# A three-stage attention, expert and feed-forward kernel: reciprocals spread in two parts, rings of their own for the sums, and a list scheduler inside the kernel that sets the order of every engine

## Chip, cores and metric

The kernel runs on one core of one Trainium2 chip. The metric is device microseconds of one execution. Five engines are spoken of: TensorE (PE, whose weight loads are shown as PEld), VectorE (DVE), ScalarE (ACT), GpSimd (POOL) and SyncE (SP), which issues all the transfers.

## What is computed

Three layers follow one another. The first is an attention in which two neighbouring query rows are averaged, the second a mixture of four attention experts of which each token takes two, the third a gated feed-forward block on the token and the token before it.

```python
def _attn_ref(q, k, v):                      # q, k, v: 4 x 8 x 1152 x 64
    q_pool = q.reshape(B, H, S // 2, 2, D).mean(axis=3)
    scores = scale * np.matmul(q_pool, k.transpose(0, 1, 3, 2))
    attn = np.exp(scores - np.max(scores, axis=-1, keepdims=True))
    attn = attn / (np.sum(attn, axis=-1, keepdims=True) + 1e-09)
    return np.matmul(attn, v)
def _moe_ref(x, w_gate, wq, wk, wv, wo):     # x: 4 x 576 x 512, four experts
    topk = np.argpartition(-(x @ w_gate), 2, axis=-1)[..., :2]
    ...
    for e in range(E):                       # causal attention of head width 64
        ye = a @ v @ wo[e]
        out += mask[..., None] * w[:, :, kk:kk + 1] * ye
def _moe2_ref(x, mu_k, mu_r, w_k, w_v, w_r): # x_prev: the token before
    xk = mu_k * x + (1.0 - mu_k) * x_prev
    xr = mu_r * x + (1.0 - mu_r) * x_prev
    k = np.maximum(xk @ w_k, 0.0)
    return 1.0 / (1.0 + np.exp(-(xr @ w_r))) * (k * k @ w_v)
```

## The kernel before

The 32 heads of the first layer (4 batches of 8) run one after another. A head has nine steps. A step multiplies one block of 128 keys with the 576 pooled queries (`s1_job`, lines 781 and 782, into a tile `st` of which PSUM holds two), ACT takes the exponential into `p` (line 787, ten buffers), and some steps later PE multiplies `p` with the values (line 815, into one of four PSUM tiles named `bank`). The sums over the keys are not taken by PE block by block: POOL and DVE add the nine `p` (line 797, tiles `sg` and `sv`), DVE joins both (line 801, `sa`), and PE sums over the partitions with a matrix of ones (line 831). The row maxima of the next head come from matmuls into `bank` (line 728) that DVE reduces (line 730). The operands of a later head are transposed, split into a high and a low part and staged in `sk` (`s1_prep`), from where DMAs copy them to their places (`KK<-sk`, `QQ<-sk`).

The normalisation of a head goes through DRAM. ACT copies the sums to a row of `U` (`finish2`, line 848), two DMAs bring them to 64 partitions (`sd`, line 854), DVE takes the reciprocals (line 858), one DMA writes them to `scr` (line 859), and one DMA reads them back, spread over 128 partitions (`R`, line 863). POOL then multiplies `U` with `R` into `XT` (line 871). When both heads of a pair are in `XT`, `s2_split` has ACT copy the high part (`XH<-XT`, line 64) and DVE subtract for the low part (`XL`, line 71). The expert layer of a batch runs between the steps of the next batch's heads: projections of the values and the gate (`stv`, line 280), of queries and keys (`stq`, line 347), four masked attentions (lines 474 to 503, with their own `normaliser`, whose `R` is read by one DMA at line 254), and the output projection (`sto`, line 555). The expert layer of the last batch stands alone behind the heads, with parts of the feed-forward block between its steps. The feed-forward weights are split into high and low parts ahead of time, in 20 chunks through one buffer `w3st` (`w3_split`: loaded at line 947, split by ACT and DVE in lines 960 to 990, stored at line 993, read back later). Twelve of them go through during the heads, eight behind them. At the end come nine groups of 256 tokens: `sth` (line 1175), `str` (line 1198), `stw` (line 1211).

Order: the work is written as a list of steps (`drive`) with tasks placed between them by a table of numbers `G`. A task is a list of small pieces spread evenly between a start and an end that are counted in steps; `later(n, f)` puts `f` n steps behind. `end1` 5, for one, is how many steps behind the sums `XT` is written. What is written so is then ordered anew on every engine by the framework's own scheduler; `behind` and `high_priority` in `s1_job` tie a few matmuls together for it. The engines run their queues in order, each instruction waiting for its semaphores. `U`, `sd`, `rd` and `R` of the heads and of the experts share rings of two buffers in the pool `sm`.

Of the kernel before, what the change touches and what calls it, by code (L numbers as in the profile page):

```python
# [25 lines left out]
G = {'LAG': 4, 'LO': 2, 'nf1': 2, 'nfx': 1, 'mxA': (0, 5), 'mxB': (-1.0, 5.5), 'mxC': (-3.5, 5.0), 'prA': (0.5, 5.0), 'prB': (-1.5, 2.0), 'mx0': (-4.2, 4.0), 'mx1': (-4.2, 4.0), 'vl': (0.0, 1.5), 'vs': (5.5, 1.0), 'pr0': (-3.0, 1.0), 'pr1': (-3.0, 1.0), 'ldA': (5.5, 5.0), 'ldB': (2.5, 2.0), 'ld': (1.5, 1.0), 'm2': (2.0, 3.0), 'nm': 2, 'nm2': 1, 'dup': 1, 'mid': 1, 'bc': 1, 'end': 9, 'end1': 5, 'mid2': 2, 'end2': 4, 'spl': 9, 'gate': 8, 'gate2': 2, 'w2': (2, 30), 'w3': (7, 14), 've': 'g', 'kh0': 's', 'kh1': 's', 'qh0': 's', 'qh1': 's', 'kq': 's', 'kl': 'v', 'rs': 'v', 'rl': 'v', 'ym': 'g', 'yo': 'v', 'LGe': 'v', 'p1': (5, 5, 5, 9), 'p2': (9, 9, 9), 'p3': (2,), 'p4': (9, 9, 9, 9), 'p5': (8, 8, 8, 8), 'p6': (9, 9, 9), 'po': (2, 4, 5, 9), 'add0': 'g', 'add1': 'g', 'xt': 'g', 'u1': 's', 'u2': 's', 'y2': 'v', 'yh': 's', 'yl': 'v', 'xo': 'v', 'v2': 's', 'xh': 's', 'xl': 'v', 'vvh': 's', 'vvl': 'g', 'klo': 'v', 'HB': 2, 'PB': 10, 'GRP': (2, 5, 8), 'GA': (1, 3, 5, 7), 'blk': 1, 'm2w': 2, 'order': 2, 'kdup': 0, 'L2': 4, 'O2': 1, 'a0': (5.0, 5.0), 'a1': (2.0, 2.5), 'a2': (0.0, 1.0), 'a3': (2.0, 2.0), 'r0': 2, 'NV': 2, 'NF': 2, 'ua': 'v', 'u0': 's', 'xt0': 'g', 'w3d': 8, 'w3q': (3, 27), 'WC': 1, 'kb': 1, 'kst': 1, 'qst': 0, 'CW': 512, 'wt': 'v', 'wl': 'v', 'wa': 'v', 'WB': 1, 'mxg': 4, 'hq': 's', 'hpos': (0, 1, 11, 20)}  # L26
NEG = -1.0e30

TINY = 1.17e-9

# [6 lines left out]
class Task:  # L37


    def __init__(self, start, end, atoms):  # L40
        self.start, self.end, self.atoms, self.done = start, end, atoms, 0

    def run(self, now):
        if now <= self.start:
            return
        if callable(self.atoms):
            self.atoms = self.atoms()
        n = len(self.atoms)
        want = n if now >= self.end else math.ceil(n * (now - self.start) / (self.end - self.start))
        while self.done < min(want, n):  # L50
            self.atoms[self.done]()
            self.done += 1
# [3 lines left out]
def tile_kernel(ctx: ExitStack, tc: tile.TileContext, q, k, v, w_gate, wq, wk, wv, wo,  # L56
                mu_k, mu_r, w_k, w_v, w_r, out):
    nc = tc.nc
# [3 lines left out]
    def copy(e, dst, src):  # L62
        if e == "s":
            nc.scalar.activation(dst, src, AF.Copy)  # L64
        elif e == "v":
            nc.vector.tensor_copy(dst, src)
        else:
            nc.gpsimd.tensor_scalar(dst, src, 1.0, 0.0, op0=ALU.mult, op1=ALU.add)

    def lo_of(e, dst, src, hi):  # L70
        eng[e].tensor_tensor(dst, src, hi.bitcast(F32), op=ALU.subtract)  # L71
# [30 lines left out]
    make_identity(nc, ident)  # L102
# [53 lines left out]
    def run_later(everything=False):  # L156
        while pending:
            x = min(pending, key=lambda x: x[0])
            if x[0] > now[0]:
                if not everything:  # L160
                    return
                now[0] = x[0]
            pending.remove(x)
            x[1]()

    lagged = []

    def drive(steps, tasks, drain=False, first=0):
# [4 lines left out]
        for i, st in enumerate(steps, first):  # L173
            now[0] += 1
            if st.qk:
                st.qk()
            if st.ew:
# [59 lines left out]
    def normaliser(U, gate, name):  # L237
# [8 lines left out]
        def mid():  # L246
# [4 lines left out]
            later(G["bc"], bcast)  # L251

        def bcast():
            nc.sync.dma_start(R, bass.AP(tensor=scr.tensor, offset=scr.offset, ap=[[0, D], [1, T]]))

# [199 lines left out]
    def s2_job(pp, b, e):  # L455
# [68 lines left out]
        def finish(j):  # L524
# [6 lines left out]
            mid, R = normaliser(U, GR[:, e], name)  # L531
# [8 lines left out]
            later(G["mid2"], mid)  # L540
            later(G["end2"], end)
# [216 lines left out]
    last_qk, owed = [None], []  # L758

    def behind(ins, prev):  # L760
        if prev is not None:
            tc.add_manual_dep(ins.ins, prev.ins.name,
                              mybir.DependencyInfo(mybir.DependencyClass.NoSync, mybir.DependencyReason.DATA),
                              reason="order")
        return ins

    def s1_job(hh):
# [5 lines left out]
        def make(si):  # L773
            items = [(0, si), (1, si)] if wide else [(x // NC, x % NC) for x in (2 * si, 2 * si + 1)]

            def qk():
                st = acc["st", si] = psA.tile([P, 2, 512], F32, tag="st", name=f"st1_{hh}_{si}")
                for n, (j, c) in enumerate(items):
# [3 lines left out]
                    last_qk[0] = nc.tensor.matmul(st[:, n, :HT], KB[i][0 : D + 1, ks], QB[i][0 : D + 1, cs],  # L782
                                                  start=False, stop=True)
# [20 lines left out]
            def values():  # L804
# [6 lines left out]
                with tc.high_priority():  # L811
                    prev = last_qk[0]
                    for x in range(si, lo, -1):
                        for j in range(2):
                            prev = behind(nc.tensor.matmul(  # L815
                                a[j * D : (j + 1) * D, :HT], V[:, x, 0:D], ps[x][:, j],
                                start=si == GRP[0] and x == si, stop=si == NC - 1 and x == lo + 1), prev)
                    if si == GRP[0]:
                        while owed:
                            owed.pop(0)(prev)  # L820
                if si == NC - 1:
                    owed.append(total)
                    U = acc["U"] = sm.tile([P, T], F32, tag="U", name=f"U1_{hh}")
                    copy("s", U[:, :HT], a[:, :HT])
                    if hh == NH - 1:
                        owed.pop(0)(last_qk[0])

            def total(prev):
                s = aux()
                for j in range(2):  # L830
                    prev = behind(nc.tensor.matmul(s[j * D : (j + 1) * D, :HT], ones, sums["all"][:, j],  # L831
                                                   start=True, stop=True), prev)
                finish2(s)
# [12 lines left out]
        def finish2(s):  # L846
            U = acc["U"]
# [9 lines left out]
            def mid():  # L857
                nc.vector.reciprocal(rd, sd)
                nc.sync.dma_start(scr.rearrange("o (p i) -> (o p) i", p=D), rd)
                later(G["bc"], bcast)  # L860
# [12 lines left out]
            later(G["mid"], mid)  # L873
            later(G["end1"], end)
# [63 lines left out]
    def w3_split(first, end, pool, bufs):  # L938
        def chunk(src, n):
# [54 lines left out]
            return [ld, sp1, sp2, sp3, sp4, sp5, sp6, sp7]  # L994
# [34 lines left out]
    for hh in range(NH):  # L1029
# [16 lines left out]
        if b and h == 1:  # L1046
            tasks.append(Task(ex_[hh][2] + G["gate"] - 2, ex_[hh][2] + G["gate"] - 1, s2_gate(c)))
        if b and h in (2, 4, 5, 6):
            tasks.append(Task(at_[hh][0] + G["m2"][0], max(at_[hh][0] + G["m2"][0] + G["m2w"], ex_[hh][0] - G["m2"][1]), s2_max(c, max(h - 3, 0))))
# [17 lines left out]
    for hh in range(NH):  # L1067
        z = "0" if hh < H else "1"
        if hh + 1 < NH:
# [4 lines left out]
            tasks.append(Task(at(hh, mx[0]), e, s1_max(hh + 1)))  # L1074
            a = LAG + G["vl"][0]
            tasks.append(Task(at(hh, a), at(hh, a + G["vl"][1]), lambda hh=hh: s1_vload(hh + 1)))
        if hh + 2 < NH:
            pr = G["pr" + z] if hh > 1 else G["prB"] if hh else G["prA"]
            tasks.append(Task(at(hh, pr[0]), at(hh, pr[1]), lambda hh=hh: s1_prep(hh + 2)))
        if hh + 3 < NH:  # L1080
            ld = G["ld"] if hh > 1 else G["ldB"] if hh else G["ldA"]
            tasks.append(Task(at(hh, ld[0]), at(hh, ld[1]), lambda hh=hh: s1_load(hh + 3)))
# [3 lines left out]
    tasks.append(Task(*G["w2"], w2_split()))  # L1086
    tasks.append(Task(at_[H][0] + G["w3"][0], n - G["w3"][1], w3_split(0, W3 // CW - G["w3d"], s1a, G["WB"])))
# [290 lines left out]
```

## Time and profile before

| | |
|---|---|
| runs | 1164.23, 1182.01 and 1174.4 us, median 1174.4 us |
| profiled execution | 1168.17 us, of which 1166.5 us from the first to the last instruction |
| mean granted TensorE clock | 0.931 of full speed |
| PE, DVE, ACT, POOL busy | 89%, 64%, 39%, 33% of the span |
| moved by DMA | 128.05 MB, mean 110 GB/s |

The span is what the rows below are taken from; the profiled execution lies 6.2 us under the median. A busy PE is not PE at full speed: in the stretches in which the clock is granted by half, the same work takes longer and counts as more busy time.

### The profile page before, as it was taken

To read this page: it belongs to the slowest core of one execution; us is meant where nothing else is said; L and a number is where in the kernel's file an instruction comes from. 1 tells how busy PE (TensorE), PEld (TensorE's weight loads), DVE (VectorE), ACT (ScalarE), POOL (GpSimd) and SP (SyncE) were. 2 spreads that over 40 slices of the span, in tenths; PEclk is the share of its full clock that TensorE was granted. 3 is DMA by queue.
4 is the path that set the end of the run, shared out by engine and by line. 5 is a ranking of instruction groups with operands and counts; after the bars stand their busy time and mean duration, and the time that the engine had idled before them with its cause. 6 is when DMAs were issued, how large, how long until landed. Compare 5 with 4: busy or idle time off the path is not lost. (4 is left out here: it accounts for less than half of the span.)

```text
span 1166.5 us, 17687 instructions
## 1 busy us (share of the span) xinstructions
PE 1032.9 (89%) x6186; PEld 811.2 (70%) x6186; DVE 743.9 (64%) x1501; ACT 456.9 (39%) x823; POOL 383.3 (33%) x483
## 2 busy tenths in 40 slices
PE   6998877879988789998889899998788899999998
PEld 4765555657666567766667776766776678888887
DVE  5676655576769577786867766684587644444432
ACT  5334334334445433453543434453256322222221
POOL 5156345233334442453433244434212101111110
PEclk9999888889899898998989888997889989999999
DMA  5656464445454474654536455316626421111100
GB/s 132 145 122 143 103 135 107 111 119 118 119 140 111 105 188 118 134 134 119 138 84 180 126 124 120 74 38 190 179 83 194 137 84 37 37 37 37 43 31 19
DMA packets 139655, 128.05 MB, mean 110 GB/s; under 512 B 64741, under 2 KB 103838, under 8 KB 139566
## 3 DMA queue, kind: packets, MB, share of 16 engines
q1 hardware_dynamic: 139566, 126.92, 43.8%
q8 instruction: 49, 0.80, 0.3%
q14 instruction: 40, 0.33, 0.1%
HBM read 63.24 MB, written 20.07 MB: 71 GB/s over the span
## 5 line engine op out<-in xcount | busy, mean ns | idle before, releaser
L730 DVE TENSOR_REDUCE PM<-bank 128x1 f32<-128x384 f32 (+1 forms) x390 | 205.9, 548 | 85.4 <-PE bank L728 83.6
L787 ACT ACTIVATE p<-st 128x576 f32<-128x576 f32 x288 | 184.7, 649 | 135.9 <-PE st L782 129.8
L781 PE MATMUL st<-QQ,KK 128*128 128x288 f32 x576 | 190.1, 341 | 17.4 <-ACT p L787 15.2
L728 PE MATMUL bank<-KK,QQ 128*128 128x384 f32 (+1 forms) x390 | 153.7, 419 | 42.4 <-DVE PM L730 17.7
L782 PE MATMUL st<-QQ,KK 65*128 65x288 f32 x576 | 178.3, 321 | 5.8 <-DMA QQ<-mr 5.2
L797 POOL TENSOR_TENSOR sg<-sg,p 128x576 f32<-128x576 f32 x90 | 137.1, 1523 | 117.4 <-ACT p L787 69.1
L815 PE MATMUL bank<-p,VF 128*64 128x288 f32 x1080 | 165.3, 448 | 0.0
L781 PEld LDWEIGHTS st<-QQ,KK 128*128 128x128 f32 x576 | 118.9, 207 | 41.1 <-ACT p L787 29.1
L728 PEld LDWEIGHTS bank<-KK,QQ 128*128 128x128 f32 (+1 forms) x390 | 77.6, 204 | 77.3 <-DVE PM L730 29.5
L782 PEld LDWEIGHTS st<-QQ,KK 65*128 65x128 f32 x576 | 119.8, 208 | 13.9 <-DMA QQ<-mr 5.9
L815 PEld LDWEIGHTS bank<-p,VF 128*64 128x64 f32 x1080 | 76.0, 148 | 60.2 <-issue 26.4
L871 POOL TENSOR_TENSOR XT<-U,R 64x288 f32<-64x288 f32 x60 | 49.9, 831 | 159.4 <-DMA R<-scr 140.6
L1175 PE MATMUL sth<-xkh,wk 128*128 128x256 f32 x512 | 91.4, 279 | 1.2 <-ACT relu L1182 1.2
L1175 PEld LDWEIGHTS sth<-xkh,wk 128*128 128x128 f32 x512 | 78.7, 188 | 1.8 <-ACT relu L1182 1.4
L503 PE MATMUL bank<-p,V 128*65 128x288 f32 (+5 forms) x288 | 65.9, 364 | 13.1 <-ACT U L64 6.1
L1112 POOL TENSOR_SCALAR yxr<-x,omr 128x256 f32<-128x256 f32 x36 | 26.2, 744 | 140.6 <-DVE xkl L144 130.6
L1175 PE MATMUL sth<-xkl,wk 128*128 128x256 f32 x256 | 71.4, 279 | 0.0
L797 DVE TENSOR_TENSOR sv<-sv,p 128x576 f32<-128x576 f32 x60 | 55.2, 920 | 23.1 <-PE bank L831 12.9
L489 POOL TENSOR_SCALAR_AFFINE_SELECT p<-p 128x128 f32<-128x128 f32 (+1 forms) x96 | 29.3, 336 | 115.9 <-ACT p L481 90.8
L1182 ACT ACTIVATE relu<-sth 128x512 f32<-128x512 f32 x32 | 17.5, 596 | 123.2 <-PE sth L1175 122.5
L797 POOL TENSOR_TENSOR sg<-p,p 128x576 f32<-128x576 f32 x30 | 46.4, 1546 | 52.9 <-ACT p L787 50.3
L1183 DVE TENSOR_TENSOR relu<-relu 128x512 f32<-128x512 f32 x32 | 20.9, 688 | 57.9 <-ACT relu L1182 57.9
(214 smaller groups left out, 2173.1 us busy)
## 6 DMA issues: line engine op xcount, KB each, us to landing
KK<-sk SPq DMA_DIRECT2D x30, 320.0 KB
qr<-in_q_dram SPq DMA_DIRECT2D x32, 288.0 KB
kr<-in_k_dram SPq DMA_DIRECT2D x32, 288.0 KB
VF<-in_v_dram SPq DMA_DIRECT2D x32, 288.0 KB
QQ<-sk SPq DMA_DIRECT2D x60, 144.0 KB
KK<-sk SPq DMA_DIRECT2D x30, 256.0 KB
R<-scr SPq DMA_DIRECT2D x48, 144.0 KB
w3h<-w3st SPq DMA_DIRECT2D x20, 256.0 KB
```

Of the source, the lines that this page charges most:

```text
L489: nc.gpsimd.affine_select(o, o, pattern=[[1, o.shape[1]]], compare_op=ALU.is_ge, fill=0.0, base=m0, channel_multiplier=-1)
L503: nc.tensor.matmul(a[:, q0 + lo : q0 + hi], V2[:n, c, e], pt[:n, c0 + lo : c0 + hi], start=start, stop=stop)
L728: nc.tensor.matmul(ps[:n, : 3 * P], QA[i][:, t0 : t0 + n], KA[i][:, 3 * g * P : 3 * (g + 1) * P], start=True, stop=True)
L730: nc.vector.tensor_reduce(pm[:n, c, g : g + 1], ps[:n, : 3 * P], axis=AX.X, op=ALU.max)
L781: nc.tensor.matmul(st[:, n, :HT], KA[i][:, ks], QA[i][:, cs], start=True, stop=False)
L782: last_qk[0] = nc.tensor.matmul(st[:, n, :HT], KB[i][0 : D + 1, ks], QB[i][0 : D + 1, cs], start=False, stop=True)
L787: nc.scalar.activation(pt, acc.pop(("st", si))[:, :, :HT], AF.Exp, scale=1.0 / 16.0)
L797: eng[e].tensor_tensor(s, x, ps[si], op=ALU.add)
L815: prev = behind(nc.tensor.matmul(a[j * D : (j + 1) * D, :HT], V[:, x, 0:D], ps[x][:, j], start=si == GRP[0] and x == si, stop=si == NC - 1 ...
L871: eng[G["xt" if b else "xt0"]].tensor_tensor(x, y, z, op=ALU.mult)
L1112: nc.gpsimd.tensor_scalar(y[:, c], t[:, c, 0:GT], om[:, c : c + 1], 0.0, op0=ALU.mult, op1=ALU.add)
L1175: nc.tensor.matmul(st[:, f // 2, f % 2 * GT : (f % 2 + 1) * GT], w[kt][:, fs], x[:, kt], start=i == 0, stop=i == 3 * KT - 1)
```

## The change

All calls of the kernel now go to a `Recorder`, which keeps them as operations with their tiles and works out which must follow which. At the end `order` simulates the five engines with planned durations (`cost`, `transfer`) and a model of the clock, always starts the operation that can start first, takes the one written earliest when several wait (shifted by a table `RK`), and issues everything in that order, with the framework's scheduler switched off. In the listings all its instructions carry line 207. `R` of the heads is read by two DMAs of 64 partitions. `U`, `sd`, `rd` and `R` of the heads have rings of two in the pool `pp1`, so that the experts no longer share them. The pieces of `s2_split` are placed pair by pair (`xhp`) and no longer all at one step; in `w3_split` four empty pieces stand between a chunk's load and its first split, and the load may not be issued before the matmul written ahead of it. Most numbers in `G` are changed.

```diff
-G = {... 'vl': (0.0, 1.5), ... 'bc': 1, 'end': 9, 'end1': 5, 'mid2': 2, 'end2': 4, 'spl': 9, ... 'p1': (5, 5, 5, 9), ... 'w3q': (3, 27), ...}
+G = {... 'vl': (1.5, 3.0), ... 'bc': 2, 'end': 10, 'end1': 7, 'mid2': 1, 'end2': 4, 'mid3': 3, 'end3': 8, 'xhp': ((6, 1), (6, 4), (7, 6), (9, 7)), ... 'p1': (8, 8, 9, 9), ... 'w3q': (-1, 24), ... 'RK': {...}}
...
+    def order(self):
...
+        while len(done) < len(self.ops):
+            best = None
+            for e in free:
+                while later[e] and later[e][0][0] <= free[e]:
+                    _, s, op = heapq.heappop(later[e])
+                    heapq.heappush(ready[e], (s, op))
+                t = free[e] if ready[e] else later[e][0][0] if later[e] else None
+                if t is not None and (best is None or t < best[0]):
+                    best = t, e
+            t, e = best
+            op = heapq.heappop(ready[e])[1] if ready[e] else heapq.heappop(later[e])[2]
...
+            if e == "SP":
+                dma = max(dma, t + 1000) + op.work
+                end = dma + 600 + op.lat
+                lanes.append(end)
...
+    def issue(self):
+        with self.tc.manual_schedule(engines=set(ISSUE)):
+            for op in self.order():
+                for call in op.calls:
+                    call()
...
+def transfer(out, src):
+
+    size = 4 * math.prod(out.shape)
+    (a, n), (b, m) = run(out), run(src)
+    r = min(a, b, 4096)
+    k = min(max(x for x in range(1, 17) if y % x == 0) for y in (n, m))
+    dram = [isinstance(x, bass.AP) or x.tile.pool.kw.get("space") == DRAM for x in (out, src)]
+    return size / r * (87 if r == 1152 else 6 + r / 26.5 * (1 if any(dram) else 2)) / k, 700.0 if dram[1] else 0.0
...
-    nc = tc.nc
+    tc = nc = Recorder(tc)
+    ctx.callback(nc.issue)
...
-                    U = acc["U"] = sm.tile([P, T], F32, tag="U", name=f"U1_{hh}")
+                    U = acc["U"] = pp1.tile([P, T], F32, tag="U", name=f"U1_{hh}", bufs=2)
...
-            sd = sm.tile([D, T // D], F32, tag="sd", name=f"sd1_{hh}")
-            rd = sm.tile([D, T // D], F32, tag="rd", name=f"rd1_{hh}")
+            sd = pp1.tile([D, T // D], F32, tag="sd", name=f"sd1_{hh}", bufs=2)
+            rd = pp1.tile([D, T // D], F32, tag="rd", name=f"rd1_{hh}", bufs=2)
             scr = dscr.tile([1, T], F32, tag="scr", name=f"scr1_{hh}")
-            R = sm.tile([P, HT], F32, tag="R", name=f"R1_{hh}")
+            R = pp1.tile([P, HT], F32, tag="R", name=f"R1_{hh}", bufs=2)
...
             def bcast():
-                nc.sync.dma_start(R, bass.AP(tensor=scr.tensor, offset=scr.offset, ap=[[HT, 2], [0, D], [1, HT]]))
+                for j in range(2):
+                    nc.sync.dma_start(R[j * D : (j + 1) * D], scr[0:1, j * HT : (j + 1) * HT].spread([[0, D], [1, HT]]))
...
-            return [ld, sp1, sp2, sp3, sp4, sp5, sp6, sp7]
+            idle = lambda: None
+            return [nc.paced(ld), idle, idle, idle, idle, sp1, sp2, sp3, sp4, sp5, sp6, sp7]
...
     for b in range(1, B):
-        tasks.append(Task(at(b * H, LAG + G["spl"]), at(b * H, LAG + G["spl"] + 1), s2_split(b - 1)))
+        for f, (i, j) in zip(s2_split(b - 1), G["xhp"]):
+            tasks.append(Task(at((b - 1) * H + i, j), at((b - 1) * H + i, j) + 0.5, [f], "h"))
```

The number of instructions on PE, DVE and ACT is the same in both; SP issues 60 DMAs `R<-scr` of 64x288 in place of 30 of 128x288.

The first place is ACT's queue in head 5, where the high part of heads 2 and 3 (`XH<-XT`) stands between the exponentials `p_5_n` of that head's steps. Before:

```order
L787 ACTIVATE p_5_3_1421<-st_5_3_1416 128x576
L64 ACTIVATE U_4_1433<-bank_1285 128x288
L787 ACTIVATE p_5_4_1440<-st_5_4_1435 128x576
L64 ACTIVATE XH<-XT 128x576
L787 ACTIVATE p_5_5_1451<-st_5_5_1446 128x576
L138 ACTIVATE mr_6_1462<-bank_1461 5x128
```

And now, in the same head:

```order
L207 ACTIVATE p_5_6_1423<-st_5_6_1414 128x576
L207 ACTIVATE p_5_7_1431<-st_5_7_1420 128x576
L207 ACTIVATE XH<-XT 128x576
L207 ACTIVATE U_4_1325<-bank_1442,eps 65x288
L207 ACTIVATE mr_6_1459<-bank_1453 5x128
L207 ACTIVATE p_5_8_1469<-st_5_8_1455 128x576
```

`XH<-XT` has moved from behind the fifth to behind the eighth exponential of head 5. The copy of head 3's sums, from which its `R` is made, stood five exponentials ahead of it before and stands ten ahead of it now.

The second place is SP's queue around the read of head 3's reciprocals (`R_3`), with the copies of a later head's operands (`QQ` and `KK` from `sk`) around it. Before:

```order
L711 DMA QQ_176<-sk_1283 64x2x288
L863 DMA R_3_1299<-scr_3_1298 128x1x288
L712 DMA QQ_176<-sk_1283 64x288
L668 DMA KK_175<-sk_1283 64x2x640
L669 DMA KK_175<-sk_1283 64x640
```

And now:

```order
L207 DMA scr_3_1295<-rd_3_1290 64x9
L207 DMA R_3_1319<-scr_3_1295 64x288 x2
L207 DMA VF_128<-in_v_dram 128x9x64
L207 DMA kr_1339<-in_k_dram 128x576
L207 DMA QQ_292<-sk_1283 64x2x288
L207 DMA KK_138<-sk_1283 64x2x512
```

`R_3` stood behind three of the `QQ` copies and now stands ahead of the first one, in two parts.

The third place is PE's queue in head 17, where the value projection of the second batch (`stv`) begins, which needs the high and low parts of all four pairs. Before:

```order
L728 MATMUL bank_4504<-KK_173,QQ_174 128x384
L781 MATMUL st_17_4_4516<-QQ_172,KK_171 128x288
L782 MATMUL st_17_4_4516<-QQ_172,KK_171 128x288
L728 MATMUL bank_4524<-KK_173,QQ_174 128x384
L280 MATMUL stv_0_4527<-wvg_h,XH 128x260
L280 MATMUL stv_0_4527<-wvg_h,XL 128x260
```

And now, the piece in which its first tile is taken up again after its first ten matmuls:

```order
L207 MATMUL stv_2_4559<-wvg_h,XL 128x260
L207 MATMUL bank_4575<-p_17_2_4462,VF_130 64x288 x2
L207 MATMUL bank_4575<-p_17_1_4440,VF_130 64x288 x2
L207 MATMUL bank_4575<-p_17_0_4426,VF_130 64x288 x2
L207 MATMUL bank_4582<-sa_16_4453,ones 64x288 x2
L207 MATMUL stv_0_4536<-wvg_h,XL 128x260
```

`stv` began behind step 4 of head 17 and now begins behind step 7; the matmuls that need the low part of the last pair stand behind eight of the second tile, six of the values and two of the sums.

## Rows read from the trace of the kernel before

**Rows 1.** Busy time in three stretches: engine us (instructions), clock, DMA share, GB/s.

```profile
40.00:835.00 795.00, 694.61 (x4235) 0.91 0.53 126
...
835.00:950.00 115.00, 98.64 (x598) 83.79 (x599) 80.18 (x184) 52.29 (x92) 16.14 (x37) 0.91 0.43 137
950.00:1166.50 216.50, 211.91 (x1248) 186.19 (x1246) 91.14 (x138) 52.54 (x77) 31.40 (x48) 1.00 0.11 35
```

**Rows 2.** The same view, an undisturbed stretch and one stall (PE, PEld, DVE, ACT, POOL).

```profile
470.00:510.00 40.00, 37.54 (x242) 27.03 (x242) 29.51 (x63) 19.71 (x37) 16.88 (x22) 1.00 0.59 126
...
130.00:140.00 10.00, 7.51 (x33) 4.91 (x33) 3.85 (x6) 4.08 (x8) 4.78 (x5) 0.66 0.12 24
```

**Rows 3.** PE's waits: us in total, times, longest us.

```profile
PE bank L728 <- DVE PM L730: 17.7, 16, 5.5
PE st L781 <- ACT p L787: 15.2, 10, 5.2
PE stv L280 <- ACT p L787: 7.5, 2, 3.9
PE bank L728 <- DMA KK<-sk: 6.3, 3, 3.3
PE bank L503 <- ACT U L64: 6.1, 1, 6.1
...
PE st L782 <- DMA QQ<-mr: 5.2, 2, 3.4
PE bank L728 <- ACT U L133: 5.1, 3, 3.0
...
PE stv L280 <- ACT XH L64: 4.8, 2, 3.3
...
PE bank L728 <- ACT U L64: 3.3, 1, 3.3
```

**Rows 4.** Waits of POOL and of ACT for the reciprocals, same columns.

```profile
POOL XT L871 <- DMA R<-scr: 140.6, 27, 9.6
...
ACT XH L64 <- POOL XT L871: 39.9, 9, 6.9
...
ACT U L133 <- POOL XT L871: 20.5, 4, 6.1
```

**Rows 5.** Timeline in head 5: start us, us, what [idle before <-releaser].

```profile
114.61 0.66 PE L831 MATMUL bank<-sa,ones 128*64 128x288 f32 x4
...
121.99 0.59 SPq L863 DMA_DIRECT2D R<-scr  x1
...
129.44 1.63 POOL L871 TENSOR_TENSOR XT<-U,R 64x288 f32<-64x288 f32 x2 [3.65 <-DMA R<-scr]
131.10 0.68 ACT L64 ACTIVATE XH<-XT 128x576 fp32r<-128x576 f32 x1 [4.62 <-POOL XT L871]
...
132.38 0.61 PE L781 MATMUL st<-QQ,KK 128*128 128x288 f32 x1 [4.94 <-ACT p L787]
```

**Rows 6.** Timeline, the experts' read of reciprocals: issue and first reader.

```profile
403.20 0.49 SPq L254 DMA_DIRECT2D R<-scr  x1
407.00 0.75 DVE L536 TENSOR_TENSOR U<-U,R 64x576 f32<-64x576 f32 x1 [0.85 <-DMA R<-scr]
...
914.40 0.46 SPq L254 DMA_DIRECT2D R<-scr  x1
917.49 0.75 DVE L536 TENSOR_TENSOR U<-U,R 64x576 f32<-64x576 f32 x1 [2.28 <-DMA R<-scr]
```

**Rows 7.** Timeline, a chunk of feed-forward weights.

```profile
239.32 0.33 SPq L947 DMA_DIRECT2D w3st<-in_moe_w_k_dram  x1
...
244.08 0.43 DVE L961 TENSOR_SCALAR w3st<-w3st 128x512 int32<-128x512 int32 x1 [3.38 <-DMA w3st<-in_moe_w_k_dram]
...
245.03 1.15 PE L728 MATMUL bank<-KK,QQ 128*128 128x384 f32 x2 [5.53 <-DVE PM L730]
```

**Rows 8.** Timeline, the last chunk behind the heads.

```profile
932.75 0.50 PE L1211 MATMUL stw<-XH,KH 128*128 128x512 f32 x1 [3.60 <-DMA XH<-w3h]
```

More of the change, by code (lines that the diff above doesn't have):

```diff
@@ L1 @@
+import heapq
 import math
-from contextlib import ExitStack
+import re
+from contextlib import ExitStack, contextmanager
+import numpy as np
 import concourse.bass as bass
@@ new lines, with __init__, place, before @@
+class Tile(View):
+    GRIDS = {}
+    def __init__(self, pool, shape, dtype, kw, prev):
+        shape = tuple(shape)
+        if shape not in Tile.GRIDS:
+            Tile.GRIDS[shape] = np.arange(math.prod(shape), dtype=np.int32).reshape(shape)
+        super().__init__(self, Tile.GRIDS[shape], dtype)
+        self.row = math.prod(shape[1:])
+        self.pool, self.kw, self.prev = pool, kw, prev
+        self.written, self.read, self.at = [], [], None
+    def place(self):
+        if self.at is None:
+            self.at = self.pool.at.tile(list(self.shape), self.dtype, **self.kw)
+        return self.at
+    def before(self):
+        t = self.prev
+        while t is not None and not t.written:
+            t = t.prev
+        return t.written + t.read if t else ()
@@ new lines, in run @@
+def run(x):
+    first, ap = None, [list(y) for y in x.ap] if isinstance(x, bass.AP) else None
+    if ap is None and any(p[0] == "spread" for p in x.path):
+        ap = [list(y) for y in x.path[-1][1][0]]
+    if ap is None:
+        ap = [[s // 4, c] for s, c in zip(x.idx.strides, x.idx.shape)]
+        if x.tile.pool.kw.get("space") != DRAM:
+            first, ap = ap[0][1], [[0, 1]] + ap[1:]
+    r = 1
+    for s, c in reversed(ap):
+        if c > 1:
+            if s != r:
+                break
+            r *= c
+    if first is None or first == 1:
+        first = next((c for s, c in ap if c > 1), 1)
+    return 4 * r, first
@@ L530, in finish @@
                 return
-            mid, R = normaliser(U, GR[:, e], name)
+            early = b < B - 1
+            mid, R = normaliser(U, GR[:, e], name, early)
             def end():
@@ L538, in end @@
                 lo_of(G["yl"], YL[o0 : o0 + D, e // 2], y[o0 : o0 + D], YH[o0 : o0 + D, e // 2])
-            later(G["mid2"], mid)
-            later(G["end2"], end)
+            later(G["mid3" if early else "mid2"], mid)
+            later(G["end3" if early else "end2"], end)
         return [make(si) for si in range(3)]
@@ L757, in tile_kernel @@
     NH = B * H
[L758 to L765, printed above, removed]
+    owed = []
     def s1_job(hh):
@@ L871, in end @@
                     eng[G["xt" if b else "xt0"]].tensor_tensor(x, y, z, op=ALU.mult)
-            later(G["mid"], mid)
-            later(G["end1"], end)
+            later(G["mid"] if late else 1, mid)
+            later(G["end1"] if late else 5, end)
         def finish(j):
```

319 lines of the change are left out of this document (276 added, 43 removed).

## Prediction

> **What bounds the kernel now.** I read the busy time by stretches first, because a mean over the span would mix three stages. In [rows 1] the reader is to see that the tail behind 950 us is solid: 211.91 of 216.5 us of PE at a granted clock of 1.00. The change leaves that order alone, so I carry the tail over. The loss lies in the 795 us of the heads: PE is busy for 694.61 us, so 100.4 us are idle, and its clock is 0.91, so 694.61 x 0.09 = 62.5 us of the busy time are lost to the half clock. The work itself is 632 us at full clock. The stretch of 115 us behind it loses 16.4 us idle and 98.64 x 0.09 = 8.9 us of clock.
>
> That the two losses hang together is seen in [rows 2]: a stretch without a long stall keeps the clock at 1.00 (37.54 of 40 us busy), and the ten microseconds with one stall of 4.94 us have 0.66, that is 7.51 x 0.34 = 2.55 us lost. So a stall costs 2.55 / 4.94 = 0.52 of its own length again; over the whole stretch the ratio is 62.5 / 100.4 = 0.62. I take 0.55.
>
> Then PE's waits [rows 3], for what ends the idle time. PE waits for ACT's exponentials and copies, but ACT is not the bottleneck. Its own waits [rows 4] lead on: ACT stands at `XH<-XT` for POOL (39.9 us, 9 times), and POOL at `XT` for the read of `R` (140.6 us, 27 times). ACT's queue is in order, so the exponentials behind `XH` come late, and PE with its two `st` tiles stops. The timeline in head 5 shows the whole chain [rows 5]: the sums of head 3 begin at 114.61, `R` is issued at 121.99, POOL starts at 129.44 (7.45 us later), `XH` at 131.10, PE again at 132.38 after 4.94 us idle. The trace has eight such gaps, in the heads behind 3, 5, 7, 13, 15, 21, 23 and 29: 4.94, 5.24, 3.34, 6.09, 3.90, 3.25, 3.65 and 2.58 us, 33.0 us together.
>
> **The change part by part.** *The read of `R`.* The same 144 KB are read by the experts as 64 rows, and there the first reader starts 3.80 and 3.09 us after the issue [rows 6]. The two halves are 64 rows each, of half the length, and the second is issued some 0.6 us behind the first (the issue in [rows 5] takes 0.59). The trace of before has no such half. Bounds: below, 3.1 us, if the two go side by side like the experts' read; above, 7.45 + 0.6 = 8.0 us, if each half takes what the whole took. I take 3.8 + 0.6 = 4.4, since the experts' read is the nearest row in bytes and partitions: 3.05 us less than now.
>
> [...]
>
> *The place of `XH`.* Counted in ACT's listing from a head's copy of its sums to `XH`, the exponentials between them go from 5 to 10 (head 3), 5 to 9, 7 to 8, 1 to 3, 7 to 5, 2 to 2, 7 to 5 and 2 to 4 (heads in the order of the gaps). A step is some 2.2 us (19.4 us between the sums of two heads without experts, by nine). Order alone then closes 4.94, 5.24 and 2.58 fully, takes 2.2 of 3.34 and 4.4 of 6.09, leaves 3.25, and could lengthen 3.90 and 3.65, where PE's listing has the matmuls that need the last pair later too. Subtracting another 3.05 us from what remains leaves 0, 0, 0, 0, 0.9, 0.2, 0.6 and 0. I allow twice that. In [rows 3] these gaps, with the copies of `U` behind the same ACT queue, are 15.2 + 7.5 + 6.1 + 4.8 + 3.3 = 36.9 us; I let 4 stay: **-33 us** idle.
>
> *Own rings.* ACT waits four times, 20.5 us, to write an expert's `U` until POOL has read a head's [rows 4], and PE three times for that copy, 5.1 us [rows 3]. With rings apart that wait has no cause: **-5**. The price is space only. Late next would be the `R` of the experts themselves, and it is the fast one.
>
> *Four empty pieces behind a weight load.* In [rows 7] `w3st` is issued at 239.32, DVE stands at line 961 for it until 244.08, and behind that the row maxima (`PM`) come late: PE idles 5.53 us. With a second, of 2.34 us at 296, and less without the usual small wait, this is some 7 of the 17.7 us of `PM`. Four pieces are several microseconds, more than the 3.38 us that DVE waited: **-7**. The load may not leave early now, which costs nothing while the four pieces cover 4.8 us.
>
> *SP's order.* The operands `KK` and `QQ` were late five times, 6.3 + 5.2 = 11.5 us [rows 3]. `R` now goes ahead of a block of these copies, but 30 issues of some 0.6 us are added, and loads of later heads stand in between, so I count half: **-6**. Bounds: -11.5 and +6.
>
> *The stretch behind the heads.* PE there waits for the weight chain, the last time 3.60 us [rows 8]. It still has one buffer, so the chunks still follow one another. Better placed pieces may take a quarter of the 25.3 us: **-6** in time; bounds 0 and -15.
>
> *The new order as such.* POOL's three added operations are a matter of nothing beside its third of the span. Of the 100.4 us idle the waits above name 36.9 + 5.1 + 17.7 + 11.5 = 71.2; the other 29 are small waits, which an order by durations can trim or add to. I take **-6** in time, bounds +25 (nearly as many again) and -25.
>
> Sum: idle -33 - 5 - 7 - 6 = -51; clock 51 x 0.55 = -28; behind the heads -6; small waits -6; together -91. 1166.5 - 91 = 1075.5 us of span, and 1.7 us outside it (1168.17 - 1166.5): **1077 us**. The profiled execution was 0.5% under the median of 1174.4, against which verdicts are taken: -8.3%.
>
> **The rivals.** *First, nothing but the steady state is left.* If the whole of the heads came to look like the undisturbed stretch [rows 2], with 6.15% idle at full clock, 632 us of work would take 632 / 0.9385 = 673 us instead of 795: -122, with -6 behind the heads 1040 of span, **1041 us**. For it: nothing else in [rows 1] is near its limit. Against it: the expert stretches have more small waits than that one.
>
> *Second, the two-part read is no faster.* 128 short rows in 7.45 and 64 long ones in 3.80 us fit a price per row as well as one per shape, and the halves have 128 rows in all. Then only order helps: of the eight gaps 19 us close and some 4 come back, A is -15, with the others -33 idle, clock -18, -6 behind the heads: 1109.5, **1111 us**.
>
> *Third, the other side: the planner's arrivals are too early.* It takes a transfer to land some time after its issue, and fixes five in-order queues on that. The framework's order has PE waiting for `KK` and `QQ` five times in 29 heads [rows 3]; if the fixed order starts a row-maximum matmul at each head as soon as the plan says that `KK` is there, PE and all behind it wait each time. A microsecond idle costs 1.55 with the clock, so the -91 are gone at 91 / 29 / 1.55 = 2.0 us per head, and it is slower by over 2% from some 2.7 us per head. With 3.3 us, the longest `KK` wait, 29 x 3.3 x 1.55 = 148 - 91 = +57: **1225 us**. For it: POOL waits up to 9.6 us for a DMA now [rows 4]. Against it: the operands are staged heads ahead, and most arrive with room.
>
> *Fourth, the stall moves to the sums' banks.* Sums are copied and spread a step or two later (`bc` 1 to 2, `end1` 5 to 7), so one of the four banks may be held longer; the wait of a row-maximum matmul for the copy of `U`, once 3.3 us now [rows 3], would come at nearly every head. At 1.7 us per head, 29 x 1.7 x 1.55 = 76 of the 91 are given back: 1151.5 of span, some **1153 us**. Against it: the bank is released by the copy, not by the read of `R`, and only the read and what follows it are moved by these two numbers.
>
> **How the numbers follow.** The forecast gets 0.55, the first rival 0.17, the second 0.14, the fourth 0.08, the third 0.06. The range takes the first and most of the second in: the bounds of the small waits (+25 and -25), of the read (+34 by the second rival) and of SP's order give 1035 to 1130. A measurement of this kernel tells about 2% from no change, that is 1151 and 1198 us around the median. Faster by more: 0.55 + 0.17 + 0.14 = 0.86; within: 0.08; slower: 0.06.
>
> **What would show it.** In the changed kernel's timeline POOL's `XT` should start 4 to 5 us after the first issue of `R`, and POOL's total wait for `R` should halve; at 7 us and more the second rival holds. ACT's wait at `XH` should fall from 39.9 to under 10 us, its wait at the experts' `U` for POOL be gone, and PE's waits for exponentials be 5 us or less in all. The heads should take some 710 us, with a clock of 0.95 or more. The tail should still take about 216 us. Waits of PE for `KK` or `QQ` over 20 us would speak for the third rival, waits for copies of `U` at nearly every head for the fourth. The forecast is wrong if idle time in the heads is above 75 us or below 30, or if the clock stays at 0.91 although the long stalls are gone.

## The result and the profile after

The changed kernel takes 1089.7 us (median of four runs, 1087.19 to 1096.19) against 1178.2 us (with a fourth run of the kernel before, of 1184.06 us), ratio 0.933 with a 95% interval of 0.923 to 0.943: faster by 6.7%. The forecast was 1077 us, with 1035 to 1130 as its range; the profiled execution of after has a span of 1094.2 us.

The kernel before is called before, and the changed kernel after. The busy time by stretches is cut where the last head's values end, where the last output projection of the experts ends, and at the span's end (PE, PEld, DVE, ACT, POOL, then clock, DMA share and GB/s). In before the cuts lie at 812 and 950 us:

```profile
40.00:812.00 772.00, 677.68 (x4126) 504.32 (x4124) 535.67 (x1097) 326.84 (x603) 310.10 (x354) 0.92 0.53 123
812.00:950.00 138.00, 115.57 (x709) 99.32 (x708) 93.03 (x206) 58.57 (x102) 22.56 (x45) 0.90 0.48 149
```

The same view of after:

```profile
40.00:730.00 690.00, 636.70 (x4112) 480.61 (x4111) 527.43 (x1089) 322.67 (x602) 319.47 (x359) 0.97 0.56 136
730.00:880.00 150.00, 124.95 (x727) 106.61 (x726) 95.88 (x211) 57.72 (x102) 25.23 (x47) 0.86 0.43 143
880.00:1094.20 214.20, 209.51 (x1229) 184.56 (x1227) 91.14 (x138) 52.55 (x77) 31.39 (x48) 1.00 0.11 37
...
130.00:140.00 10.00, 9.91 (x64) 6.70 (x61) 6.07 (x13) 3.80 (x8) 0.71 (x1) 0.89 0.26 53
```

The heads gained 82 us: PE idles 53 us there instead of 94, and is busy for 41 us less. The stretch behind them, the last batch, lost 12 us, and the tail, from which a few matmuls moved ahead, gained 2. The ten microseconds that had the stall of 4.94 us [rows 2] are full now, though other work stands there.

The waits of after that answer to [rows 3, 4] (us in total, times, longest):

```profile
POOL XT L207 <- DMA R<-scr: 69.7, 19, 12.1
...
DVE rd L207 <- DMA sd<-U: 43.1, 27, 4.3
...
PE bank L207 <- DVE PM L207: 11.1, 19, 2.6
...
PE st L207 <- ACT p L207: 8.2, 15, 1.6
PE st L207 <- DMA QQ<-ml: 7.8, 7, 1.9
PE bank L207 <- DMA QQ<-sk: 5.8, 5, 2.4
...
PE st L207 <- DMA QQ<-mr: 4.8, 5, 3.3
...
PE bank L207 <- DMA KK<-sk: 2.7, 2, 2.0
...
ACT relu L207 <- POOL XT L207: 7.0, 1, 7.0
...
PE stv L207 <- ACT p L207: 0.9, 2, 0.5
...
ACT XH L207 <- POOL XT L207: 0.6, 1, 0.6
```

POOL's wait for `R` has halved, ACT's wait for POOL at `XH` has gone from 39.9 to 0.6 us, and no wait of PE for an exponential is longer than 1.6 us (5.1 us of them lie in the heads). Two waits have grown: that of DVE for `sd`, from 6.4 us in 6 places, and those of PE for `KK` and `QQ`, from 11.9 us to 21.1 us, all in the heads. The timeline answers to [rows 5]:

```profile
118.89 1.12 SPq L207 DMA_DIRECT2D R<-scr  x2
...
123.12 2.08 POOL L207 TENSOR_TENSOR XT<-U,R 64x288 f32<-64x288 f32 x2
```

POOL starts 4.2 us after the first issue and hasn't waited for the transfer. Where it did wait, in 19 places of after, the median from the issue of `R` to POOL's start is 2.73 us; in before it was 7.36 us over the 27 places.

### The profile page after: what moved, and what is told of

It reads as the page before. It is cut to its first block, busy times and chain, and to the rows that moved or that the text cites. A ratio compares the mean times of both kernels' runs of the same rounds, so it can differ in the third digit from the quotient of the medians.

```text
span 1094.2 us, 17703 instructions
## 1 busy us (share of the span) xinstructions
PE 999.0 (91%) x6186; PEld 792.5 (72%) x6186; DVE 738.8 (68%) x1501; ACT 451.9 (41%) x823; POOL 391.0 (36%) x483
## 4 chain that ended last, share of the span: by engine, by line
PE 60%; DMA 15%; DVE 13%; ACT 5%; SPq 3%; issue 2%; POOL 0%; DVEq 0%; ACTq 0%; POOLq 0%
PE bank L207 21%; PE st L207 12%; PE stw L207 9%; PE sth L207 8%; PE str L207 5%; DVE PM L207 4%; DMA sd<-U 4%; PE stq L207 4%; SPq L207 3%; DVE w3st L207 2%; DMA QQ<-ml 2%; PE stv L207 2%; DMA w3st<-in_moe_w_k_dram 2%; DMA scr<-rd 2%; DMA QQ<-sk 2%
## 5 line engine op out<-in xcount | busy, mean ns | idle before, releaser
L207 DVE TENSOR_REDUCE PM<-bank 128x1 f32<-128x384 f32 (+3 forms) x466 | 239.3, 541 | 57.8 <-PE bank L207 56.0
L207 ACT ACTIVATE p<-st 128x576 f32<-128x576 f32 (+2 forms) x352 | 213.5, 622 | 150.9 <-PE st L207 135.2
L207 PE MATMUL st<-QQ,KK 128*128 128x288 f32 (+1 forms) x1152 | 243.3, 325 | 24.2 <-DMA QQ<-ml 7.8
L207 PEld LDWEIGHTS st<-QQ,KK 128*128 128x128 f32 (+1 forms) x1152 | 187.9, 198 | 57.1 <-ACT p L207 13.7
L207 PE MATMUL bank<-p,VF 128*64 128x288 f32 (+1 forms) x1152 | 176.4, 422 | 0.8 <-ACT p L207 0.7
L207 PEld LDWEIGHTS bank<-p,VF 128*64 128x64 f32 (+1 forms) x1152 | 80.3, 138 | 57.9 <-issue 14.5
L207 PE MATMUL sth<-xkh,wk 128*128 128x256 f32 x576 | 109.4, 288 | 6.7 <-ACT relu L207 3.9
L207 POOL TENSOR_TENSOR XT<-U,R 64x288 f32<-64x288 f32 (+1 forms) x62 | 57.5, 928 | 72.9 <-DMA R<-scr 69.7
L207 PEld LDWEIGHTS sth<-xkl,wk 128*128 128x128 f32 x288 | 56.5, 196 | 0.3
L207 POOL TENSOR_TENSOR qp<-qr 96x384 f32<-96x384 f32 x31 | 35.9, 1157 | 46.2 <-PE bank L207 42.1
```

The costliest lines, as they stand in the source:

```text
L207: getattr(getattr(self.tc.nc, name), method)(*real, **{k: x.real() if isinstance(x, View) else x for k, x in kw.items()})
```

## The experiments

Ratios are to runs of the kernel before that were taken together with those of the edited kernel. Times within a run are from one profiled execution, so a difference of a few us between two of them is weak evidence. "Stretch behind" is the span less the end of the heads: 354 us in before (1166.5 - 812.1), 364 us in after (1094.2 - 730.2).

**The two-part read alone, and all but the read.** First the kernel before with one edit:

```diff
-                nc.sync.dma_start(R, bass.AP(tensor=scr.tensor, offset=scr.offset, ap=[[HT, 2], [0, D], [1, HT]]))
+                for j in range(2):
+                    nc.sync.dma_start(R[j * D : (j + 1) * D], bass.AP(tensor=scr.tensor, offset=scr.offset + j * HT, ap=[[0, D], [1, HT]]))
```

> The kernel before, with R of the heads read by two DMAs of 64 partitions and nothing else changed. Theory of the forecast (the read's shape is a main cause): POOL's XT starts 4 to 5 us after the issue instead of 7.45, the eight gaps shrink from 33 to some 9 us, and with the clock the time falls by some 37 us, ratio 0.97. Rival 'order alone' (the planner's order, not the read, made the gain): the XT starts earlier, but the time stays within 1%, ratio 0.99 to 1.01. Rival 'two parts no faster': XT still 7 us or more after the issue.

Measured: 1094.1 us, ratio 0.929 (0.925 to 0.934). One edit gives what the whole change gives, twice what was expected of it. Its waits, and its heads (PE's busy time alone, then clock, DMA share and GB/s):

```profile
PE bank L728 <- DVE PM L730: 10.6, 12, 2.9
...
PE st L781 <- ACT p L787: 7.6, 13, 1.5
...
PE st L782 <- DMA QQ<-ml: 1.5, 4, 0.7
...
POOL XT L872 <- DMA R<-scr: 34.2, 13, 5.6
...
ACT XH L64 <- POOL XT L872: 17.7, 9, 3.2
```

```profile
40.00:741.00 701.00, 650.06 (x4126) 0.96 0.55 136
```

The heads lose 43 us of idle time, not the 24 of the eight gaps: PE's waits for `KK` and `QQ<-mr` have gone too (11.5 us in [rows 3]), and those for the row maxima fell by 7. ACT still waits 17.7 us at `XH`, and the gain is there all the same. The stretch behind is 352 us.

Then the changed kernel with the old read:

```diff
-                for j in range(2):
-                    nc.sync.dma_start(R[j * D : (j + 1) * D], scr[0:1, j * HT : (j + 1) * HT].spread([[0, D], [1, HT]]))
+                nc.sync.dma_start(R, scr.spread([[HT, 2], [0, D], [1, HT]]))
```

> The changed kernel with R of the heads read by one DMA of 128 partitions as before; the planner plans for it. Theory of the forecast: some 34 us slower than the changed kernel, about 1124 us, ratio to before 0.957. Rival 'order alone': the planner places the multiplication far enough behind the read, so within 10 us of the changed kernel, ratio 0.93 to 0.94.

Measured: 1151.5 us, ratio 0.979 (0.976 to 0.983). All the rest of the change is worth some 2% on the slow read, and nothing that can be measured on the fast one (0.933 against 0.929). "Order alone" falls: ACT waits only 3.9 us at `XH` in this run, and it is slow all the same. By stages the rest does two things. It shortens the heads, which end at 774 instead of 812 us on the slow read and at 730 instead of 741 us on the fast one, and it lengthens the stretch behind them, to 378 from 354 us and to 364 from 352 us. In this run ACT stands there for the last `XT`, and PE behind it for 14.0 us:

```profile
ACT relu L207 <- POOL XT L207: 15.9, 1, 15.9
```

**The shape or the number of parts.** In the kernel before, one DMA of 128 rows of the same length, whose source has an outer dimension of 128:

```diff
-                nc.sync.dma_start(R, bass.AP(tensor=scr.tensor, offset=scr.offset, ap=[[HT, 2], [0, D], [1, HT]]))
+                nc.sync.dma_start(R, bass.AP(tensor=scr.tensor, offset=scr.offset, ap=[[0, P], [1, HT]]))
```

> The kernel before, with R read by one DMA of 128x288 whose source has an outer dimension of 128 (step 0) instead of 2; both halves of the partitions get the first half's reciprocals, so the upper half of XT is scaled by the wrong ones. Theory 'the source's outer dimension of 2 is what is slow': XT starts at most 4.5 us after the issue and the time is that of the kernel before with the two-part read, within 1%: 1083 to 1105 us, ratio 0.92 to 0.94. Rival 'the rows' (128 short rows cost 7 us whatever the dimension, and two queued halves only overlap): 7 us and more to XT, ratio 0.99 to 1.01.

Measured: 1102.7 us, ratio 0.939 (0.934 to 0.945). Over the 22 places where POOL waited, the median from issue to start is 3.67 us, against 7.36 of the old read with the same rows and bytes:

```profile
POOL XT L871 <- DMA R<-scr: 48.8, 22, 6.8
```

So neither the 128 rows nor the single DMA was slow, but the source's outer dimension of 2. Two parts are somewhat earlier still (2.76 us, 13 places).

**What the slow read did to the others.** The two-part read, and behind it the old one into a tile that nobody reads:

```diff
+                idle = pp1.tile([P, HT], F32, tag="idle", name=f"idle_{hh}", bufs=2)
+                nc.sync.dma_start(idle, bass.AP(tensor=scr.tensor, offset=scr.offset, ap=[[HT, 2], [0, D], [1, HT]]))
```

> The kernel before with the two-part read, and behind it, per head, the old read of 128x1x288 into a tile that nothing reads. Theory 'the slow read also held up the other transfers' (the KK copies issued 1.8 us behind it landed 3 us behind it): POOL's XT stays early, but KK and QQ are late again, and about half of the gain is given back, 1115 to 1145 us, ratio 0.95 to 0.975. Rival 'the chain through XT alone': nobody waits for the idle read, 1090 to 1103 us, ratio 0.925 to 0.94.

Measured: 1160.0 us, ratio 0.987 (0.981 to 0.993). It gives back not half but four fifths of the gain: 55 us in the heads, which end at 796 us instead of 741, and 15 behind them. Its waits:

```profile
PE bank L728 <- DMA KK<-sk: 13.6, 5, 3.8
...
PE bank L429 <- DMA KA<-KA: 8.9, 4, 4.9
...
PE st L782 <- DMA QQ<-ml: 5.9, 4, 3.5
...
PE st L782 <- DMA QQ<-mr: 5.0, 4, 3.4
```

```profile
40.00:796.00 756.00, 677.16 (x4130) 0.92 0.54 131
```

PE waits for transfers again, more than in before, while the two-part reads themselves stay fast (median 2.86 us over 17 places). The 15 us behind the heads are partly of the idle tile's own making, for it lies in a pool that is to be closed there (PE stands 11.7 us for `relu`). The extra read also adds an issue of some 0.6 us per head on SP's queue and 144 KB of traffic; a fast read of the same size in its place was not tried. That the issues alone did it is unlikely: the two-part read adds as many and gained.

The traces show the link itself, in the times at which a transfer's landings are counted on its semaphore. All 30 slow reads of before have three such counts: one at 1.0 us after the issue, and two at the end, the last at 7.3 us (medians). The reads of the two other shapes have sixteen, as all 60 halves of after have. The transfers that SP issued within 1.9 us behind a slow read have fourteen counts and then, 4.5 us later, the last two (median of 58 in before; behind the idle read 4.5 us, 68 transfers). Behind the two-part read the last two come 0.16 us after the fourteenth (65 transfers), and 0.13 us in after (41 transfers). So of the sixteen landings of a transfer behind the slow read two come 4.5 us late, and the reader waits for those.

**Own rings.** In the kernel before, `U`, `sd`, `rd` and `R` of the heads in `pp1`, two buffers each:

```diff
-            R = sm.tile([P, HT], F32, tag="R", name=f"R1_{hh}")
+            R = pp1.tile([P, HT], F32, tag="R", name=f"R1_{hh}", bufs=2)
```

> The kernel before with own rings of two for U, sd, rd and R of the heads, nothing else. Theory of the forecast: the waits of ACT at the experts' U for POOL (20.5 us) go, PE's 5.1 us behind them too; with the clock -8 us, ratio 0.993. Rival: the copies wait for something else and nothing is gained, ratio 1.00.

Measured: 1183.1 us, ratio 1.004 (1.001 to 1.008), slower if anything. ACT's wait at the experts' `U` for POOL is gone, but a new one stands behind the heads:

```profile
ACT relu L1244 <- POOL XT L871: 16.2, 1, 16.2
```

The undoing in the changed kernel (all four back in `sm`):

> The changed kernel with U, sd, rd and R of all heads back in the rings of sm that the experts use. Theory of the forecast: PE waits again for the copy of U at row maxima, some 8 us slower, 1098 us, ratio 0.94. Rival 'own rings only lengthen the last batch': the first of the last eight weight loads leaves earlier and the time from the heads' end to the last instruction falls from 364 to 352 to 357 us, 1078 to 1086 us, ratio 0.92 to 0.928.

Measured: 1116.4 us, ratio 0.948 (0.944 to 0.951). There the own rings are worth some 1.6% (0.948 / 0.933), more than forecast: 16 us in the heads, which end at 746 instead of 730 us. The stretch behind did not get shorter but longer: 370 us. PE's wait for the copy of `U`, which the forecast named, comes back with 2.1 us only, so what the rest of the 16 us is stays open. Both theories miss: the rings matter where the order was written for them, and cost a little where it wasn't.

**The wait behind the heads.** In after four engines start together when the last head's `XT` is written:

```profile
746.53 1.65 POOL L207 TENSOR_TENSOR XT<-U,R 64x288 f32<-64x288 f32 x2 [4.53 <-DMA R<-scr]
748.21 0.35 SPq L207 DMA_DIRECT2D w3st<-in_moe_w_v_dram  x1
748.22 0.60 ACT L207 ACTIVATE relu<-sth 128x512 f32<-128x512 f32 x1 [6.95 <-POOL XT L207]
748.22 0.76 DVE L207 COPY xo<-sto 128x576 f32<-128x576 f32 x1 [5.59 <-POOL XT L207]
...
748.87 0.58 PE L207 MATMUL sth<-xkh,wk 128*128 128x256 f32 x1 [3.90 <-ACT relu L207]
```

`relu` and `w3st` lie in the pool `s3`, which gets the memory of the heads' pools once these are closed, and `pp1` closes with the last reader of `R`. An edit lets the last two heads use `sm`:

```diff
-            R = pp1.tile([P, HT], F32, tag="R", name=f"R1_{hh}", bufs=2)
+            R = (pp1 if hh < NH - 2 else sm).tile([P, HT], F32, tag="R", name=f"R1_{hh}", bufs=2 if hh < NH - 2 else None)
```

(likewise `U`, `sd` and `rd`)

> The changed kernel with U, sd, rd and R of the last two heads in the experts' rings in sm, all other heads in their own rings in pp1. Theory 'the own rings in pp1 keep the heads' pools open until the last XT, and the first of the last eight weight loads waits for that': the load leaves within 8 us of the heads' end instead of 18, the last batch's stretch is 138 to 142 us instead of 150, time 8 to 12 us under the changed kernel's 1090, ratio 0.915 to 0.926. Rival 'the planner's order of the last batch is the cause': the stretch stays at 150 us, ratio 0.93 to 0.935.

Measured: 1086.8 us, ratio 0.926 (0.921 to 0.931). The wait of `relu` is gone, and the weight load leaves 14 us behind the heads instead of 18. Expected were 8 us, and 138 to 142 us for the last batch, which takes 146. The stretch behind is 360 us, 4 of the 10 lost; the time is within noise of the changed kernel's. It is the lowest ratio measured, if not surely the lowest.

Three edits aimed at the rest of that stretch. The first takes the numbers of the last batch from before (`L2`, `O2`, `a0` to `a3`, `w3q`, `hpos` and `mid2` in `G`) and drops the empty pieces there:

```diff
-            return [nc.paced(ld), idle, idle, idle, idle, sp1, sp2, sp3, sp4, sp5, sp6, sp7]
+            if first:
+                return [ld, sp1, sp2, sp3, sp4, sp5, sp6, sp7]
+            return [nc.paced(ld), idle, idle, idle, idle, sp1, sp2, sp3, sp4, sp5, sp6, sp7]
```

> The changed kernel with the last batch's numbers of before (L2, O2, a0 to a3, w3q, hpos, mid2) and without the empty pieces and the pacing at the last eight chunks. Theory 'these numbers cost the last batch its 12 us': from the heads' end to the last instruction 352 to 356 us instead of 364, 1078 to 1083 us, ratio 0.92 to 0.925. Rival 'the own rings cost it': 362 us or more, ratio 0.93 or above.

Measured: 1098.2 us, ratio 0.932 (0.929 to 0.936). The heads end 11 us earlier, at 719 us, and the stretch behind takes 376 us: nothing won. Time and stretch lie where the rival put them, but the rings are not shown as the cause by that, since with shared rings the stretch took 370 us. Neither theory named the trade of one stretch for the other.

The second changes the number of chunks left for the last batch (`'w3d': 8` to `6`):

> The changed kernel with 14 of the 20 chunks of feed-forward weights split during the heads and 6 behind them, in place of 12 and 8 (w3d 6); nothing else. Theory 'the stretch behind the heads is bound by the chain of the last chunks through one buffer' (eight chunks from 748.2 to 853.7 us, 13.2 us each, whatever the heads do): it falls by some 26 us, from 150 to 122 to 132 us, the heads lose at most 6 us, 1066 to 1078 us, ratio 0.905 to 0.92. Rival 'the last batch's own chain of experts bounds it' (the heads' earlier end gave nothing in two runs): the stretch stays above 145 us, ratio 0.927 to 0.94.

Measured: 1118.4 us, ratio 0.953 (0.950 to 0.956). The heads grow by 25 us, with PE idle for 70 us there instead of 53, and the stretch behind falls by 3, to 361 us. The six chunks are through 98 us behind the heads' end, the eight of after 123 us, but the last output projection ends 142 us behind it instead of 149. The chain of chunks is not alone what bounds the stretch.

**Landings.** The third moves the time at which the planner counts a transfer as landed:

```diff
-                end = dma + 600 + op.lat
+                end = dma + 1600 + op.lat
```

> The changed kernel with the planner counting 1.0 us more from a transfer's issue to its landing (600 to 1600 ns behind the transfer itself); nothing else. Theory 'the planner takes transfers to land too early' (the forecast's third rival, in a small dose: DVE waits 43.1 us in 27 places for sd at the reciprocals, PE some 29 us for transfers): DVE's wait for sd falls under 15 us, PE's idle time in the heads from 51 to under 42 us, and with the clock the time falls by 10 to 25 us, 1065 to 1080 us, ratio 0.91 to 0.924. Rival 'these waits are covered': the waits shrink but the time stays within 8 us, ratio 0.926 to 0.94.

Measured: 1098.7 us, ratio 0.932 (0.928 to 0.936). The waits shrink as expected, and so do the heads, by 13 us; the stretch behind grows by more, to 383 us:

```profile
DVE rd L207 <- DMA sd<-U: 15.6, 16, 1.7
```

```profile
40.00:717.00 677.00, 635.88 (x4112) 0.97 0.58 138
717.00:888.00 171.00, 134.93 (x744) 0.82 0.39 127
```

**The planner's order.** The program of the changed kernel, in its written order, given to the framework's scheduler:

```diff
-        with self.tc.manual_schedule(engines=set(ISSUE)):
-            for op in self.order():
-                for call in op.calls:
-                    call()
+        for op in self.ops:
+            for call in op.calls:
+                call()
```

> The changed kernel with its written order handed to the framework's scheduler instead of the planner inside the kernel (two-part read, rings, empty pieces and numbers in G as changed). Theory of the forecast (the parts carry it, the planner's order as such some 6 us, at most 25): 1095 to 1120 us, ratio 0.93 to 0.955. Rival 'order alone': most of the gain is gone, 1150 us or more, ratio 0.98 or above.

Measured: 1113.4 us, ratio 0.947 (0.944 to 0.951). The heads show little idle time, but much more busy time at nearly full clock:

```profile
40.00:747.00 707.00, 673.97 (x4125) 0.99 0.55 134
...
L207 PE MATMUL bank<-p,VF 128*64 128x288 f32 (+1 forms) x1152 | 216.7, 424 | 0.7 <-DVE PM L207 0.6
```

The matmuls of the values, which overlap when they stand together (24 of them, of 410 ns each, in 3.13 us at one place of before), take 216.7 us there and 176.4 us in after. So the second version ties them as before did (`high_priority`, each behind the one ahead):

> As after_framework_order, with the matmuls of the values tied together and put at high priority, as the kernel before does for the framework's scheduler. Theory 'the planner earns only by keeping those matmuls together': PE's work in the heads falls by some 40 us, idle time stays near 32 us, and the time is at or below the changed kernel's, 1070 to 1092 us, ratio 0.91 to 0.93. Rival 'the planner's order is worth its place': 1097 us or more, ratio 0.937 or above.

Measured: 1103.8 us, ratio 0.941 (0.937 to 0.945); the values take 183.4 us. The planner's order looks some 0.8% better than that, with intervals that overlap. The comparison that does not overlap is with the kernel before plus the two-part read, under the same scheduler (0.929): the new numbers, rings, empty pieces and places cost about 1% there. The loss stands behind the heads: they end at 737.5 us against 741, and the stretch behind takes 364.5 us against 352. In the first of the two versions it takes 363 us. So the longer stretch is there without the planner's order too.

## Why the prediction was right

**The total, and the stages.** The direction and the main cause, the read of `R`, were right; that the total came so near was in good part luck. By its second rival the forecast gave the read 34 us, and the other 57 to parts that bring nothing measurable beside the fast read. The read alone brings 82. The forecast put -85 us into the heads and -6 behind them; measured are -82 and +12 in the last batch, -2 in the tail. The idle time in the heads fell by 41 us, from 94.3 to 53.3, against the 51 forecast. The busy time fell by 41, against the 28 put down for the clock: by an estimate from the clocks shown (677.68 x 0.08 = 54, 636.70 x 0.03 = 19) some 35 of them are the clock's. Two terms, too high and too low by about ten, made up for each other. That work takes longer at a lower clock is seen in before: ten matmuls of the values keep PE busy for 2.6 us in 462.2 to 465.4 us, at 0.50, and 24 of them for 3.1 us in 311.3 to 314.5 us, at 1.00. (The 1040 us of span of the first rival should be 1038.5, by 1166.5 - 122 - 6; nothing rests on it.)

**The read of `R`: right step, mis-sized.** The forecast counted the read as 3.05 us faster through the chain by `XT` and `XH`, worth 24 us of idle in before and some 34 us in the changed kernel. It starts earlier than the forecast's 4.4 us and than its lower bound of 3.1: 2.73 us in after. Undone, it costs 5%; done alone, it brings 7%. The sum had no term for what the slow read did to the transfers behind it, and booked their delays elsewhere: to SP's order, to the empty pieces. The rows of before show it at one place:

```profile
145.41 0.58 SPq L863 DMA_DIRECT2D R<-scr  x1
...
147.25 0.60 SPq L669 DMA_DIRECT2D KK<-sk  x1
...
152.57 1.65 POOL L871 TENSOR_TENSOR XT<-U,R 64x288 f32<-64x288 f32 x2 [3.75 <-DMA R<-scr]
...
155.57 0.66 PE L728 MATMUL bank<-KK,QQ 128*128 128x384 f32 x1 [3.29 <-DMA KK<-sk]
```

The last `KK` copy was issued at 147.25 us, 1.8 us behind `R`. Fourteen of its sixteen landings were counted by 150.89 us, the last two at 155.39 and 155.43, 2.9 us behind those of `R` at 152.44 and 152.51; PE started at 155.57. The run with the idle read shows that the link holds without POOL or ACT.

**The halves against the whole.** That two halves start the reader sooner than the whole was the author's estimate from the experts' read, 3.80 us in [rows 6]. In the kernel before the two halves took 2.76 us, and one DMA of 128 rows with an outer dimension of 128 at its source 3.67 us, against 7.36 us of the old read. Sixteen landings are counted for the first two and three for the old one. A price per row, for which the second rival spoke, does not fit the 3.67 us.

**The order.** ACT's wait at `XH` is gone, as the counts of exponentials said, but little hung on it: it is 3.9 us in the run with the old read, which is slow, and 17.7 us in the run with the two-part read alone, which is fast. The second rival, in which only order helps, was priced at 1111 us, and the run with the old read took 1151.5.

**Own rings, -5.** Right in direction under the planner (undone, 1.6% slower), wrong under the old order, and "the price is space only" is what failed: the rings in `pp1` hold the memory of the last batch until the last read of `R`, a wait of ACT of 7.0 us in after, 15.9 with the old read and 16.2 in the run with rings alone.

**Empty pieces, -7, and SP's order, -6.** In the kernel before with nothing but the two-part read, most of what these two were to bring had come already (row maxima 17.7 to 10.6 us, no more waits for `KK` worth a row), so the slow read was at least part of their cause. SP's order went the other way: PE's waits for `KK` and `QQ` in the heads are 11.9 us in before, 1.5 us with the two-part read alone, and 21.1 us in after.

**Behind the heads, -6: wrong.** It is +12 in the last batch. One part has a cause that was shown, the pool that closes late: its wait went with the ring, and the stretch with it by 4 us, of one profile each. The rest stays open: under the framework's scheduler the stretch is as long, with the heads ended earlier (717 and 719 us) it grew, and with fewer chunks it hardly shrank. The planner's order, the weight chain and the numbers of the last batch do not explain it alone.

**The third rival, in a small dose.** The planner does take transfers to land too early: DVE waits 43.1 us for `sd`, and PE 21.1 us for `KK` and `QQ`, over the 20 us that the forecast had set as this rival's sign. Later landings brought PE's waits for `KK` and `QQ` down to 9.3 us and took 13 us out of the heads, so such waits are not free there, but the time did not change. The rival's price, 3.3 us at every head on PE, did not come: there were 19 such waits, most of them under 2 us.

## What to carry to other kernels

When a small transfer is slow, look at the outer dimension of its source before its bytes (7.36 us with 2 there and 3.67 us with 128, for the same 144 KB); and ask what is queued behind it (here two of sixteen landings 4.5 us late), since the waits that it causes elsewhere carry the names of other tiles. Test a change of many parts by its smallest part on the old kernel first: here one edit of two lines carried all that could be measured. A ring in a pool that is to be closed keeps what reuses its memory waiting until the ring's last reader (ACT for 16.2 us in the run with rings alone).

## What was not expected of the hardware

A read of 144 KB whose source has an outer dimension of 2 took 7.36 us to its reader, and 3.67 us with 128 there, by the same rows and bytes. Thirty such reads into a tile that nobody reads made the heads 55 us longer: the last two of sixteen landings of the transfers behind one come 4.5 us late, although the DMAs of the core are busy for only half of the time by the mean (share 0.54 in that run's heads). And the clock did not rise at one rate with the idle time that went: by an estimate from the clocks shown, 28 us of busy time for 43 us of idle in the run with the read alone (0.92 to 0.96), 35 for 41 in after (0.92 to 0.97).
